# Attention, gated projection and channel MLP on one core: the values' weight conversion at one word operation a step, the exchange of halves added in place, and the last pair's reciprocals a step later

## The chip, the core and the metric

The kernel runs on one core of a Trainium2 chip. The core has a matrix engine (TensorE, PE in the profile, its weight loads PEld), a vector engine (VectorE, DVE), an engine for functions of one input (ScalarE, ACT), a general engine (GpSimd, POOL) and SyncE (SP), which here issues DMAs. Each engine works through its own queue in order; where an instruction needs another engine's result or a buffer that another still reads, it waits, and everything behind it in that queue waits too. The metric is the device time of one execution in microseconds.

## What is computed

The reference chains three blocks on two batches of 768 positions and 512 channels:

```python
q_bits = (np.einsum('bhsd,dk->bhsk', q, proj) > 0)   # 6 bits a row, the same for k
mask = q_bucket[:, :, :, None] == k_bucket[:, :, None, :]
scores = np.where(mask, scale * (q @ k.T), -1e9)
attn = exp(scores - max); attn = attn / (sum(attn) + 1e-9); x = attn @ v
...
val = x @ w_val                                       # gated by a 5-tap convolution of x
x = (gate * val) @ w_out
...
u = x + real(fft2(x)); un = normalise(u)
out = u + relu(un @ w_ch1) @ w_ch2
```

The weights (w_val, w_out, w_ch1, w_ch2, conv_w) arrive as 64-bit numbers. The kernel takes them apart by operations on their 32-bit words into a high and a low part, which TensorE multiplies one after the other.

## The kernel before

The profile has three stages: attention to about 253 us, the gated projection and the Fourier mixing to 344 us, the channel block to the end. The change is in the attention stage (function `attention`).

Attention goes over eight pairs of heads, p = 0 to 7, and in each over twelve blocks of 128 queries, i = 0 to 11 (two heads of six). A loop over n = 12p + i writes the instructions down in the order in which every engine runs them; nothing reorders them later. One turn of the loop is a step. In step n TensorE transposes the exponentials of block n (ptp), does the scores of block n + 3 (sp, four matmuls, L557), and half of a product with the values (op, L616: step by step one half of a 256-query group kb, so that one group ends every second step). VectorE clamps the scores of block n + 3 to SBUF and takes their minimum (L568), and forms the low part of the transposed exponentials (ptl, L605), after ScalarE has copied the high part (pth, L601). ScalarE also does the exponential of block n + 2 (L575).

Other work is spread over the steps i of a pair:

- `qk_beside`: at i = 1 to 3 and 9 to 11 two transposes of a later pair's queries and keys; ScalarE writes ht (L698), VectorE lt (L701). Six DMAs (L411 to L416: four qk<-ht, two qk<-lt) place them into qk at i = 3 and 9, and the next turn of ht can be written only after these have read it.
- the hash bits at i = 4 and 5: projections on TensorE (L443), signs on VectorE (L454), scaling on GpSimd (L458).
- the values of a later pair, on GpSimd at i = 5 and 11 (L174, L389, L174).
- the word operations of one half of a block of w_val (`val_weights`, through `half_weights` and `words_split`) at i = 6 to 10, in pair 0 at i = 7 to 11, in the last pair at i = 0 to 4. step0 is two operations on VectorE (L271, L272) into the PSUM tile cvp, step1 one (L275), step2 one on ScalarE and two on VectorE (L279, L280), step3 one (L283), step4 one copy on ScalarE. The tile cvp stands in the pool psm.
- the exchange of halves, at the end of each group kb (`pv_out`): two heads share the 128 partitions, and the high and low products of a head stand in different halves. ScalarE copies the group to xc (L629, two buffers), a DMA brings the other half to xs (L633, one buffer), and GpSimd adds both into xm (L634) a step after. So the DMA of a group waits for the add of the group before, and a copy to xc for the add two groups back.
- the reciprocals of the row sums (`norm_spread` on VectorE, L644; `norm_beside`: transposed on TensorE, L666, at i = 4, in the last pair at i = 1; through a DMA to rs, `norm_rows`; `norm_mul` on GpSimd, L719, at i = 10, in the last pair at i = 5).
- the convolution's products and sums of finished pairs, on GpSimd (L239, L241).

The line that says when a group is added:

```python
if kb - 1 in add and part == 0:
    add.pop(kb - 1)()
```

CW lists the steps n at which the conv weights' conversion runs.

Of the kernel before, what the change touches and what calls it, by code (L numbers as in the profile page):

```python
# [10 lines left out]
F32 = mybir.dt.float32  # L11
F32R = mybir.dt.float32r
AF = mybir.ActivationFunctionType
ALU = mybir.AluOpType
I32 = mybir.dt.int32
I64 = mybir.dt.int64

P = 128
B, H, S, D = 2, 8, 768, 64
DM = H * D  # L20
# [9 lines left out]
KSCALE = -0.125  # L30
BIG = 2.0 ** 33

CW = (2, 3, 4, 4, 5, 6, 7, 12)

WARM = (18, 3, 4)
CLAMP = BIG / 4
# [68 lines left out]
def block_kernel(  # L105
# [4 lines left out]
    nc = tc.nc  # L110
# [8 lines left out]
    col = cpool.tile([P, 6], F32, name="col")  # L119
# [60 lines left out]
    xs, gs = ExitStack(), ExitStack()  # L180
# [3 lines left out]
    g = [gpool.tile([P, NC, S + 1], F32, name=f"g{b}") for b in range(B)]  # L184
# [4 lines left out]
    wvh = xpool.tile([P, NC, DM], F32R, name="wvh")  # L189
    wvl = xpool.tile([P, NC, DM], F32R, name="wvl")  # L190
# [66 lines left out]
    ap4 = pool(raws, "ap4", side="right")  # L257
    pso = pool(ws, "pso", psum=True)
    psm = pool(ws, "psm", psum=True)
    wo_raw, wo_h, wo_l = {}, [None] * NC, [None] * NC  # L260

    def words_split(raw, dst_h, dst_l, b, a, g):

        n = raw.shape[1]
        words = raw.bitcast(I32).rearrange("p (n two) -> p n two", two=2)
        lo, hi = words[:, :, 0], words[:, :, 1]
        a, g = a.bitcast(I32), g.bitcast(I32)
        e = ap4.tile([P, DM], I32, tag="cve", name="cv")[:, :n]

        def step0():  # L270
            nc.vector.tensor_scalar(a, hi, 0x7FFFFE00, None, op0=ALU.bitwise_and)  # L271
            nc.vector.tensor_scalar(g, hi, 0x1FF, 15, op0=ALU.bitwise_and, op1=ALU.logical_shift_left)  # L272

        def step1():
            nc.vector.scalar_tensor_tensor(g, lo, 17, g, op0=ALU.logical_shift_right, op1=ALU.bitwise_or)  # L275

        def step2():
            nc.scalar.activation(a, a, AF.Relu, scale=8.0, bias=col[:, b : b + 1])
            nc.vector.scalar_tensor_tensor(a, hi, -(2 ** 31), a, op0=ALU.bitwise_and, op1=ALU.bitwise_or)  # L279
            nc.vector.tensor_scalar(e, a, -(2 ** 23), None, op0=ALU.bitwise_and)  # L280

        def step3():
            nc.vector.scalar_tensor_tensor(dst_l, g, 2.0 ** -35, e.bitcast(F32), op0=ALU.mult, op1=ALU.mult)  # L283

        def step4():
            nc.scalar.copy(dst_h, a.bitcast(F32))

        return [step0, step1, step2, step3, step4]

    def half_weights(raw, dst_h, dst_l, b):  # L290
        t = psm.tile([P, DM], F32, tag="m", name="cvp")
        n = DM // 2
        return words_split(raw, dst_h, dst_l, b, t[:, :n], t[:, n:])

    def out_load(c):

# [5 lines left out]
    def attention(es):  # L302
# [4 lines left out]
        ap2 = pool(es, "ap2", 2)  # L307
# [5 lines left out]
        NPR = len(pairs)  # L313
# [307 lines left out]
        def pv_out(kb):  # L621
            p, j, blk = kb // 6, (kb % 6) // 3, kb % 3
            if kb % 6 == 0:
                st[p]["xm"] = ap2.tile([P, S], F32, tag="xm", name="xm")
            mr = slice(64 * j, 64 * j + 64)
            cr = slice(64 - 64 * j, 128 - 64 * j)
            xc = ap2.tile([P, QB], F32, tag="xc", name="xc")
            xs = ap2.tile([P, QB], F32, tag="xs", name="xs", bufs=1)
            nc.scalar.copy(xc, po[kb])  # L629
            if kb == 6 * NPR - 1:  # L630
                nc.scalar.copy(xs[mr, :], po[kb][cr, :])
            else:
                nc.sync.dma_start(xs[mr, :], xc[cr, :])  # L633
            add[kb] = lambda: nc.gpsimd.tensor_tensor(  # L634
                st[p]["xm"][mr, blk * QB : (blk + 1) * QB], xc[mr, :], xs[mr, :], op=ALU.add
            )

        def norm_sums(p):
            sums = st[p]["sums"]
# [67 lines left out]
        def beside(p, i):  # L707

            if p + 2 < NPR and i >= 9:
                return qk_beside(p + 2, 0, i - 9)  # L710
            if 1 <= p and p + 1 < NPR and 1 <= i < 4:
                return qk_beside(p + 1, 1, i - 1)
            if 1 <= p and i == (1 if p == NPR - 1 else 4):
                return norm_beside(p - 1)

        def norm_mul(p):
# [60 lines left out]
        def val_weights(i):  # L777
            c, h = divmod(i, 2)
            cs = slice(h * DM // 2, (h + 1) * DM // 2)
            return half_weights(wv_raw[i], wvh[:, c, cs], wvl[:, c, cs], 3)  # L780

        def out_tile(i):
            t = qk_tile((0, 2, 1)[i]).rearrange("p a s -> p (a s)")
# [19 lines left out]
        for n in range(NT + 2):  # L803
# [28 lines left out]
                pv_out(kb)  # L832
            if n == 6:
                prep_step(1, i)
            if kb - 1 in add and part == 0:
                add.pop(kb - 1)()
            elif n == NT + 1:
                add.pop(kb)()
            if n == 0:
                values(0, 1)  # L840
# [8 lines left out]
            if i == 0 and p + 1 < NPR:  # L849
                load_v(p + 1)  # L850
            last = p == NPR - 1
            if i == (2 if last else 7) and 1 <= p < NPR:
                norm_rows(p - 1)
            if i == (5 if last else 10) and 1 <= p < NPR:
                norm_mul(p - 1)
            if n == NT - 1:
                early = pst.tile([P, 2, 512], F32, tag="t", name="early")
# [19 lines left out]
            elif n == NT - 2:  # L877
                norm_spread(p)

            at = 0 if last else 7 if p == 0 else 6  # L880
            if p < NPR and at <= i < at + 5:
                if i == at:
                    wsteps = val_weights(p)
                    if p + 1 < NPR:
                        val_load(p + 1)
                wsteps[i - at]()
            for _ in range(1 if n >= NT - 16 else 5 * n // 6 - 5 * (n - 1) // 6):
                if convs and n < NT and n >= min(12 * (4 * convs[0][0] + convs[0][1]) + 22, NT - 6):
                    conv_pool(*convs.pop(0), conv_tmp)
# [547 lines left out]
```

## Time and profile before

| | |
|---|---|
| time, median of three runs | 616.01 us (615.88, 616.01, 618.68) |
| profiled execution | 617.74 us, its span 616.0 us |
| TensorE busy | 603.3 us, 98% |
| VectorE busy | 444.9 us, 72% |
| ScalarE busy | 359.0 us, 58% |
| GpSimd busy | 269.7 us, 44% |

Busy shares are means over all three stages: VectorE's tenths are 9 in most of the attention stage and 1 in most of the channel stage. In the chain that ended last TensorE has 73% and VectorE 15%. A line of a timeline gives the start, the duration, the engine, the line of the kernel and the tiles; durations of consecutive instructions of one engine overlap a little, so the distance of two starts is what an instruction takes of its queue. In square brackets stands the idle time ahead of it, if any, and what ended it.

### The profile page before, as it was taken

Reading aid. Unit: us, or ns where it says so; the run is one execution under the profiler, and the core shown is the slowest. Engines: PE = TensorE matmul, PEld = TensorE weight load, DVE = VectorE, ACT = ScalarE, POOL = GpSimd, SP = SyncE. Lnnn points to the kernel's source line nnn. Section 1 sums busy time; section 2 is a strip of 40 time slices with the busy share of each in tenths; the row PEclk is TensorE's granted clock in tenths of the full one; section 3 lists DMA queues with packets and bytes.
Section 4 is the critical chain, followed back from the end, with each engine's and each line's share of the span. In section 5 each row is a group of like instructions: output and inputs, shape, how many; then the busy total and the mean of one; then the engine's idle time right before and its main releaser. Section 6 shows DMA issues by size and latency. Waiting matters only on the chain.

```text
span 616.0 us, 10435 instructions
## 1 busy us (share of the span) xinstructions
PE 603.3 (98%) x3711; PEld 539.0 (87%) x3711; DVE 444.9 (72%) x850; ACT 359.0 (58%) x712; POOL 269.7 (44%) x303
## 2 busy tenths in 40 slices
PE   8999999999999999999999999999999999999997
PEld 6889999999899989998899978888888888888886
DVE  5999999999899998799769888888886411111113
ACT  5998899998899887954625255555666111111221
POOL 7252488887798899793350632332331000000000
PEclk9999999999999999999999999999999999999999
DMA  6957585756566640162110234433440200000002
GB/s 136 219 134 171 134 185 153 173 149 158 149 159 157 196 125 14 47 257 70 36 35 0 66 122 124 135 119 122 137 136 1 103 0 1 2 0 1 0 1 102
DMA packets 54957, 62.02 MB, mean 101 GB/s; under 512 B 29184, under 2 KB 42664, under 8 KB 54650
## 3 DMA queue, kind: packets, MB, share of 16 engines
q1 hardware_dynamic: 54170, 57.81, 35.0%
q0 software_dynamic: 432, 3.55, 1.5%
q8 instruction: 29, 0.48, 0.3%
q14 instruction: 22, 0.18, 0.1%
q10 hardware_dynamic: 304, 0.01, 0.0%
HBM read 36.73 MB, written 3.19 MB: 65 GB/s over the span
## 4 chain that ended last, share of the span: by engine, by line
PE 73%; DVE 15%; ACT 3%; DMA 3%; issue 2%; SPq 2%; POOL 1%; ACTq 0%; DVEq 0%; POOLq 0%
PE pf L1344 20%; PE acc L1354 20%; PE sp L557 7%; PE op L616 6%; PE ptp L593 5%; DVE sd L568 4%; DVE ptl L605 4%; PE ps L1161 3%; PE ps L222 3%; PE ps L1225 2%; DMA qk<-ht 2%; PE late L222 1%; PE early L222 1%; PE ptp L693 1%; PE bp L443 1%
## 5 line engine op out<-in xcount | busy, mean ns | idle before, releaser
L1354 PE MATMUL acc<-w,hid 128*128 128x512 f32 x576 | 136.9, 390 | 0.0
L1354 PEld LDWEIGHTS acc<-w,hid 128*128 128x128 f32 x576 | 105.6, 188 | 19.7
L1347 DVE SCALAR_TENSOR_TENSOR hid<-pf,hid 128x512 fp32r<-128x512 f32 (+1 forms) x62 | 33.4, 557 | 119.5 <-ACT hid L1346 119.5
L1344 PE MATMUL pf<-uth,w 128*128 128x512 f32 (+1 forms) x496 | 96.7, 337 | 0.1
L568 DVE TENSOR_SCALAR_CACHE_REDUCE sd<-sp 128x768 f32<-128x768 f32 x96 | 91.2, 951 | 7.6 <-PE sp L557 7.1
L605 DVE TENSOR_TENSOR ptl<-ptp,pth 128x768 fp32r<-128x768 f32 x96 | 91.6, 954 | 5.8 <-ACT pth L601 3.8
L557 PE MATMUL sp<-qk 128*128 128x512 f32 (+1 forms) x384 | 91.5, 360 | 4.2 <-DVE sd L568 3.2
L1346 ACT ACTIVATE hid<-pf 128x512 fp32r<-128x512 f32 (+1 forms) x62 | 28.9, 488 | 114.0 <-PE pf L1344 113.9
L1344 PEld LDWEIGHTS pf<-uth,w 128*128 128x128 f32 x496 | 79.4, 188 | 14.4 <-DVE hid L1347 2.0
L575 ACT ACTIVATE sd<-sd,nm 128x768 f32<-128x768 f32 x96 | 90.1, 939 | 1.5 <-DVE sd L568 1.5
L601 ACT CAST pth<-ptp 128x768 fp32r<-128x768 f32 x96 | 77.1, 803 | 17.6 <-PE ptp L693 8.8
L162 POOL TENSOR_TENSOR w<-cv 128x512 fp32r<-128x512 f32 x31 | 40.1, 1295 | 88.7 <-DVE cv L157 77.3
L593 PE MATMUL ptp<-ident,sd 128*128 128x128 f32 x576 | 78.5, 272 | 0.2 <-ACT sd L575 0.2
L616 PE MATMUL op<-pth,v 128*128 128x256 f32 x288 | 74.0, 283 | 1.5 <-ACT xc L629 1.5
L616 PE MATMUL op<-ptl,v 128*128 128x256 f32 x288 | 73.8, 286 | 0.0
L557 PEld LDWEIGHTS sp<-qk 128*128 128x128 f32 x384 | 58.2, 189 | 13.7 <-DVE sd L568 7.3
L593 PEld LDWEIGHTS ptp<-ident,sd 128*128 128x128 f32 x576 | 65.8, 140 | 1.1 <-ACT sd L575 0.5
L634 POOL TENSOR_TENSOR xm<-xc,xs 64x256 f32<-64x256 f32 x48 | 35.3, 735 | 57.3 <-DMA xs<-xc 34.7
L616 PEld LDWEIGHTS op<-pth,v 128*128 128x128 f32 x288 | 54.1, 188 | 6.4 <-ACT xc L629 2.6
L616 PEld LDWEIGHTS op<-ptl,v 128*128 128x128 f32 x288 | 54.2, 188 | 0.3
L1344 PE MATMUL pf<-utl,w 128*128 128x512 f32 (+1 forms) x248 | 52.8, 335 | 0.0
L149 ACT ACTIVATE cv<-cv,col 128x512 int32<-128x512 int32 x32 | 23.3, 727 | 41.5 <-DVE cv L146 41.5
(214 smaller groups left out, 1000.9 us busy)
## 6 DMA issues: line engine op xcount, KB each, us to landing
raw<-in_moe_w_ch_dram SPq DMA_DIRECT2D x32, 512.0 KB
qk<-ht SPq DMA_DIRECT2D x60, 192.0 KB
qk<-lt SPq DMA_DIRECT2D x30, 192.0 KB
rqk<-in_q_dram SPq DMA_DIRECT2D x16, 192.0 KB
rqk<-in_k_dram SPq DMA_DIRECT2D x16, 192.0 KB
rv<-in_v_dram SPq DMA_DIRECT2D x8, 384.0 KB
out_dram<-o SPq DMA_DIRECT2D x12, 256.0 KB
xs<-xc SPq DMA_DIRECT2D x47, 64.0 KB
```

The lines of the kernel that those rows point to most:

```text
L162: nc.gpsimd.tensor_tensor(dst()[1], fold(g.bitcast(F32)), fold(e.bitcast(F32)), op=ALU.mult)
L557: nc.tensor.matmul(sp[:, cs], q2[i][:, m, qi * P : (qi + 1) * P], k2[i][:, m, cs], start=m == order[0], stop=m == order[1])
L568: nc.vector.tensor_scalar(sd[n], sp, CLAMP, None, op0=ALU.min, op1=ALU.min, accum_out=st[p]["nm"][:, n % 12 : n % 12 + 1],)
L575: nc.scalar.activation(sd[n], sd[n], AF.Exp, bias=st[p]["nm"][:, i : i + 1], scale=-1.0, accum_out=st[p]["sums"][:, i : i + 1],)
L593: nc.tensor.transpose(tp[:, r // 3, c0 : c0 + P], sd[n][:, r * P : (r + 1) * P], ident)
L601: nc.scalar.copy(p_parts(n)[0], tp)
L605: nc.vector.tensor_tensor(lo, tp, f32(ho), op=ALU.subtract)
L616: nc.tensor.matmul(po[kb], v3[:, r, c0 : c0 + P], pt[kb][x][:, r, :], start=r == 0 and x == 0, stop=r == R - 1 and x == 1,)
L634: add[kb] = lambda: nc.gpsimd.tensor_tensor(st[p]["xm"][mr, blk * QB : (blk + 1) * QB], xc[mr, :], xs[mr, :], op=ALU.add)
L1344: nc.tensor.matmul(pf, w[:, c, :], x[:, c, :], start=n == 0, stop=n == 3 * NC - 1)
L1347: nc.vector.scalar_tensor_tensor(hl[:, cs], pf, 0.0, f32(hh)[:, cs], op0=ALU.max, op1=ALU.subtract)
L1354: nc.tensor.matmul(acc, x[:, ts_], w, start=f == 0 and n == 0, stop=f == NF - 1 and n == 2)
```

## The change

Three edits. The word operations of w_val go through `spread_weights`: six steps instead of five, with one VectorE operation each, from i = 4 on (pair 0: 5, last pair: 0), and the sixth at the next pair's i = 0. The first two write an SBUF tile cv instead of PSUM; the third reads the raw words and cv, both in SBUF, and writes cvp in PSUM. The exchange has no tile xs: the DMA writes into xm, and GpSimd adds xc to it in place, a step later (at odd i). In the last pair the reciprocals' transpose, their spread and the multiplication come a step later, and the conv weights' last step moves from n = 12 to 13.

```diff
--- before.py
+++ after.py
@@ -30,7 +30,7 @@
 KSCALE = -0.125
 BIG = 2.0 ** 33
 
-CW = (2, 3, 4, 4, 5, 6, 7, 12)
+CW = (2, 3, 4, 4, 5, 6, 7, 13)
 
 WARM = (18, 3, 4)
 CLAMP = BIG / 4
@@ -291,6 +291,45 @@
         t = psm.tile([P, DM], F32, tag="m", name="cvp")
         n = DM // 2
         return words_split(raw, dst_h, dst_l, b, t[:, :n], t[:, n:])
+
+    def spread_weights(raw, dst_h, dst_l, b):
+
+
+        n = raw.shape[1]
+        words = raw.bitcast(I32).rearrange("p (n two) -> p n two", two=2)
+        lo, hi = words[:, :, 0], words[:, :, 1]
+        w = {}
+
+        def magnitude():
+            w["s"] = ap4.tile([P, DM], I32, tag="cve", name="cv")
+            nc.vector.tensor_scalar(w["s"][:, :n], hi, 0x7FFFFE00, None, op0=ALU.bitwise_and)
+
+        def upper():
+            nc.vector.tensor_scalar(
+                w["s"][:, n:], hi, 0x1FF, 15, op0=ALU.bitwise_and, op1=ALU.logical_shift_left
+            )
+
+        def rest():
+            t = psm.tile([P, DM], F32, tag="m", name="cvp").bitcast(I32)
+            w["a"], w["g"] = t[:, :n], t[:, n:]
+            nc.vector.scalar_tensor_tensor(
+                w["g"], lo, 17, w["s"][:, n:], op0=ALU.logical_shift_right, op1=ALU.bitwise_or
+            )
+            nc.scalar.activation(w["a"], w["s"][:, :n], AF.Relu, scale=8.0, bias=col[:, b : b + 1])
+
+        def sign():
+            nc.vector.scalar_tensor_tensor(w["a"], hi, -(2 ** 31), w["a"], op0=ALU.bitwise_and, op1=ALU.bitwise_or)
+
+        def power():
+            nc.vector.tensor_scalar(w["s"][:, :n], w["a"], -(2 ** 23), None, op0=ALU.bitwise_and)
+
+        def low():
+            nc.vector.scalar_tensor_tensor(
+                dst_l, w["g"], 2.0 ** -35, w["s"][:, :n].bitcast(F32), op0=ALU.mult, op1=ALU.mult
+            )
+            nc.scalar.copy(dst_h, w["a"].bitcast(F32))
+
+        return [magnitude, upper, rest, sign, power, low]
 
     def out_load(c):
 
@@ -625,15 +664,13 @@
             mr = slice(64 * j, 64 * j + 64)
             cr = slice(64 - 64 * j, 128 - 64 * j)
             xc = ap2.tile([P, QB], F32, tag="xc", name="xc")
-            xs = ap2.tile([P, QB], F32, tag="xs", name="xs", bufs=1)
+            to = st[p]["xm"][mr, blk * QB : (blk + 1) * QB]
             nc.scalar.copy(xc, po[kb])
             if kb == 6 * NPR - 1:
-                nc.scalar.copy(xs[mr, :], po[kb][cr, :])
+                nc.scalar.copy(to, po[kb][cr, :])
             else:
-                nc.sync.dma_start(xs[mr, :], xc[cr, :])
-            add[kb] = lambda: nc.gpsimd.tensor_tensor(
-                st[p]["xm"][mr, blk * QB : (blk + 1) * QB], xc[mr, :], xs[mr, :], op=ALU.add
-            )
+                nc.sync.dma_start(to, xc[cr, :])
+            add[kb] = lambda: nc.gpsimd.tensor_tensor(to, xc[mr, :], to, op=ALU.add)
 
         def norm_sums(p):
             sums = st[p]["sums"]
@@ -710,7 +747,7 @@
                 return qk_beside(p + 2, 0, i - 9)
             if 1 <= p and p + 1 < NPR and 1 <= i < 4:
                 return qk_beside(p + 1, 1, i - 1)
-            if 1 <= p and i == (1 if p == NPR - 1 else 4):
+            if 1 <= p and i == (2 if p == NPR - 1 else 4):
                 return norm_beside(p - 1)
 
         def norm_mul(p):
@@ -777,7 +814,7 @@
         def val_weights(i):
             c, h = divmod(i, 2)
             cs = slice(h * DM // 2, (h + 1) * DM // 2)
-            return half_weights(wv_raw[i], wvh[:, c, cs], wvl[:, c, cs], 3)
+            return spread_weights(wv_raw[i], wvh[:, c, cs], wvl[:, c, cs], 3)
 
         def out_tile(i):
             t = qk_tile((0, 2, 1)[i]).rearrange("p a s -> p (a s)")
@@ -832,9 +869,9 @@
                 pv_out(kb)
             if n == 6:
                 prep_step(1, i)
-            if kb - 1 in add and part == 0:
+            if kb - 1 in add and part == (0 if kb == 6 * NPR - 1 else 1):
                 add.pop(kb - 1)()
-            elif n == NT + 1:
+            if n == NT + 1:
                 add.pop(kb)()
             if n == 0:
                 values(0, 1)
@@ -849,9 +886,9 @@
             if i == 0 and p + 1 < NPR:
                 load_v(p + 1)
             last = p == NPR - 1
-            if i == (2 if last else 7) and 1 <= p < NPR:
+            if i == (3 if last else 7) and 1 <= p < NPR:
                 norm_rows(p - 1)
-            if i == (5 if last else 10) and 1 <= p < NPR:
+            if i == (6 if last else 10) and 1 <= p < NPR:
                 norm_mul(p - 1)
             if n == NT - 1:
                 early = pst.tile([P, 2, 512], F32, tag="t", name="early")
@@ -877,13 +914,15 @@
             elif n == NT - 2:
                 norm_spread(p)
 
-            at = 0 if last else 7 if p == 0 else 6
-            if p < NPR and at <= i < at + 5:
+            at = 0 if last else 5 if p == 0 else 4
+            if 1 <= p < NPR and i == 0:
+                wsteps.pop(0)()
+            if p < NPR and at <= i < at + (6 if last else 5):
                 if i == at:
                     wsteps = val_weights(p)
                     if p + 1 < NPR:
                         val_load(p + 1)
-                wsteps[i - at]()
+                wsteps.pop(0)()
             for _ in range(1 if n >= NT - 16 else 5 * n // 6 - 5 * (n - 1) // 6):
                 if convs and n < NT and n >= min(12 * (4 * convs[0][0] + convs[0][1]) + 22, NT - 6):
                     conv_pool(*convs.pop(0), conv_tmp)
```

On VectorE in pair 3, from the first bits operation (i = 4) on; L568 and L605 are the clamp and the low part of each step, and two word operations stand together at i = 6 and i = 8. Before:

```order
L454 TENSOR_TENSOR bits<-bp,bits 64x384
L568 TENSOR_SCALAR sd,nm<-sp 128x768
L605 TENSOR_TENSOR ptl<-ptp,pth 128x6x128
L454 TENSOR_TENSOR bits<-bp,bits 64x384
L568 TENSOR_SCALAR sd,nm<-sp 128x768
L605 TENSOR_TENSOR ptl<-ptp,pth 128x6x128
L271 TENSOR_SCALAR cvp<-wvr 128x256
L272 TENSOR_SCALAR cvp<-wvr 128x256
L568 TENSOR_SCALAR sd,nm<-sp 128x768
L605 TENSOR_TENSOR ptl<-ptp,pth 128x6x128
L275 SCALAR_TENSOR_TENSOR cvp<-wvr,cvp 128x256
L568 TENSOR_SCALAR sd,nm<-sp 128x768
```

After (L493 the bits, L607 the clamp, L644 the low part):

```order
L493 TENSOR_TENSOR bits<-bp,bits 64x384
L305 TENSOR_SCALAR cv<-wvr 128x256
L607 TENSOR_SCALAR sd,nm<-sp 128x768
L644 TENSOR_TENSOR ptl<-ptp,pth 128x6x128
L493 TENSOR_TENSOR bits<-bp,bits 64x384
L308 TENSOR_SCALAR cv<-wvr 128x256
L607 TENSOR_SCALAR sd,nm<-sp 128x768
L644 TENSOR_TENSOR ptl<-ptp,pth 128x6x128
L315 SCALAR_TENSOR_TENSOR cvp<-wvr,cv 128x256
L607 TENSOR_SCALAR sd,nm<-sp 128x768
L644 TENSOR_TENSOR ptl<-ptp,pth 128x6x128
```

Each step has now one word operation: magnitude (L305), upper (L308), rest (L315) and sign (L321), the first two ahead of where the conversion began before.

On VectorE at the start of the last pair, around the reciprocals (rinv). Before:

```order
L568 TENSOR_SCALAR sd,nm<-sp 128x768
L605 TENSOR_TENSOR ptl<-ptp,pth 128x6x128
L644 RECIPROCAL rinv<-sums 128x12
L271 TENSOR_SCALAR cvp<-wvr 128x256
L272 TENSOR_SCALAR cvp<-wvr 128x256
L568 TENSOR_SCALAR sd,nm<-sp 128x768
L605 TENSOR_TENSOR ptl<-ptp,pth 128x6x128
L275 SCALAR_TENSOR_TENSOR cvp<-wvr,cvp 128x256
```

After:

```order
L607 TENSOR_SCALAR sd,nm<-sp 128x768
L644 TENSOR_TENSOR ptl<-ptp,pth 128x6x128
L681 RECIPROCAL rinv<-sums 128x12
L327 SCALAR_TENSOR_TENSOR wvl<-cvp,cv 128x256
L305 TENSOR_SCALAR cv<-wvr 128x256
L607 TENSOR_SCALAR sd,nm<-sp 128x768
L644 TENSOR_TENSOR ptl<-ptp,pth 128x6x128
L308 TENSOR_SCALAR cv<-wvr 128x256
L607 TENSOR_SCALAR sd,nm<-sp 128x768
L644 TENSOR_TENSOR ptl<-ptp,pth 128x6x128
```

The reciprocals keep their place and two word operations beside them: the sixth of pair 6 (L327) and the first of this pair (L305); the steps after have one.

On GpSimd in pair 2, around the multiplication L719 (xT<-xm,rs) at i = 10; L634 is the add, L640 the sums, conv_tmp and g_73 are the convolution's products and sums. Before:

```order
L634 TENSOR_TENSOR xm<-xc,xs 64x256
L241 TENSOR_TENSOR g_73<-g_73,conv_tmp 128x768
L640 TENSOR_SCALAR sums<-sums 128x12
L634 TENSOR_TENSOR xm<-xc,xs 64x256
L719 TENSOR_TENSOR xT_72<-xm,rs 128x6x128
L239 TENSOR_SCALAR g_73<-xT_72,cwt 128x768
L174 TENSOR_SCALAR v_1581<-rv 128x6x64
L389 TENSOR_TENSOR v_1581<-rv,v_1581 128x6x64
L174 TENSOR_SCALAR v_1581<-v_1581 128x6x64
L239 TENSOR_SCALAR conv_tmp<-xT_72,cwt 128x768
L634 TENSOR_TENSOR xm<-xc,xs 64x256
```

After (L673 the add, L756 the multiplication, L428 the values' addition):

```order
L673 TENSOR_TENSOR xm<-xc,xm 64x256
L241 TENSOR_TENSOR g_73<-g_73,conv_tmp 128x768
L673 TENSOR_TENSOR xm<-xc,xm 64x256
L677 TENSOR_SCALAR sums<-sums 128x12
L756 TENSOR_TENSOR xT_72<-xm,rs 128x6x128
L239 TENSOR_SCALAR g_73<-xT_72,cwt 128x768
L673 TENSOR_TENSOR xm<-xc,xm 64x256
L174 TENSOR_SCALAR v_1562<-rv 128x6x64
L428 TENSOR_TENSOR v_1562<-rv,v_1562 128x6x64
L174 TENSOR_SCALAR v_1562<-v_1562 128x6x64
L239 TENSOR_SCALAR conv_tmp<-xT_72,cwt 128x768
```

The adds come at other places between the other operations: one of them now follows the multiplication and the convolution's product, ahead of the values (L174, L428).

## Rows read from the trace of the kernel before

**Rows 1.** Windows: length; PE, PEld, DVE, ACT, POOL busy us (instructions); clock, DMA share, GB/s
```profile
119.00:148.00 29.00, 28.71 (x219) 27.20 (x218) 27.75 (x54) 26.17 (x55) 22.46 (x25) 1.00 0.71 170
215.00:241.00 26.00, 25.07 (x189) 23.48 (x188) 24.39 (x48) 21.32 (x44) 24.07 (x23) 1.00 0.31 79
```

**Rows 2.** Timeline, TensorE: start, duration, instruction, [idle before, what ended it]
```profile
123.44 0.82 PE L593 MATMUL ptp<-ident,sd 128*128 128x128 f32 x6
...
147.22 0.82 PE L593 MATMUL ptp<-ident,sd 128*128 128x128 f32 x6
...
149.28 0.82 PE L593 MATMUL ptp<-ident,sd 128*128 128x128 f32 x6
150.38 0.97 PE L557 MATMUL sp<-qk 128*128 128x512 f32 x4 [0.29 <-DVE sd L568]
...
151.94 0.82 PE L593 MATMUL ptp<-ident,sd 128*128 128x128 f32 x6
```

**Rows 3.** Timeline, VectorE, 148 to 152 us
```profile
148.59 0.42 DVE L271 TENSOR_SCALAR cvp<-wvr 128x256 int32<-128x256 int32 x1
...
149.37 0.95 DVE L568 TENSOR_SCALAR_CACHE_REDUCE sd<-sp 128x768 f32<-128x768 f32 x1
...
151.11 0.42 DVE L275 SCALAR_TENSOR_TENSOR cvp<-wvr,cvp 128x256 int32<-128x256 int32 x1
151.44 0.95 DVE L568 TENSOR_SCALAR_CACHE_REDUCE sd<-sp 128x768 f32<-128x768 f32 x1
```

**Rows 4.** Timelines, TensorE and, last, ScalarE, 161 to 168 us
```profile
161.16 0.82 PE L593 MATMUL ptp<-ident,sd 128*128 128x128 f32 x6
...
163.45 0.81 PE L593 MATMUL ptp<-ident,sd 128*128 128x128 f32 x6
...
166.51 0.39 PE L616 MATMUL op<-pth,v 128*128 128x256 f32 x1 [1.32 <-ACT xc L629]
...
167.33 0.82 PE L593 MATMUL ptp<-ident,sd 128*128 128x128 f32 x6
...
164.80 0.47 ACT L698 ACTIVATE ht<-ptp,col 128x256 fp32r<-128x256 f32 x1 [1.77 <-DMA qk<-ht]
```

**Rows 5.** Timeline, SyncE, 126 to 159 us: DMA issues
```profile
126.93 0.48 SPq L633 DMA_DIRECT2D xs<-xc  x1
...
158.17 0.48 SPq L633 DMA_DIRECT2D xs<-xc  x1
158.70 0.60 SPq L411 DMA_DIRECT2D qk<-ht  x1
```

**Rows 6.** Timeline, GpSimd, 157 to 164 us
```profile
157.41 0.73 POOL L634 TENSOR_TENSOR xm<-xc,xs 64x256 f32<-64x256 f32 x1 [3.36 <-DMA xs<-xc]
...
163.04 0.91 POOL L239 TENSOR_SCALAR g<-xT,cwt 128x768 f32<-128x768 f32 x1
```

**Rows 7.** Timeline, TensorE, last pair
```profile
221.44 0.27 PE L666 MATMUL ptp<-ident,rinv 128*12 128x128 f32 x1 [0.68 <-DVE rinv L644]
```

**Rows 8.** Timelines of the channel stage, VectorE and, last, GpSimd
```profile
360.41 1.51 DVE L146 TENSOR_SCALAR cv<-raw 128x512 int32<-128x512 int32 x1 [0.23 <-ACT w L169]
...
365.71 0.42 DVE L146 TENSOR_SCALAR cv<-raw 128x512 int32<-128x512 int32 x1
...
360.36 1.28 POOL L162 TENSOR_TENSOR w<-cv 128x512 fp32r<-128x512 f32 x1 [2.58 <-DVE cv L157]
```

**Rows 9.** Groups by line and form: instruction xcount, busy us, mean ns, idle us before
```profile
L1054 DVE TENSOR_TENSOR gt<-g 128x384 f32<-128x384 f32 x8 | 6.5, 849 | 2.4 <-POOL gl L1062 2.4
L1054 DVE TENSOR_TENSOR gt<-g,late 128x384 f32<-128x384 f32 x8 | 4.2, 552 | 0.3 <-POOL xT L719 0.2
```

**Rows 10.** Timelines of pair 1, VectorE and, last, GpSimd
```profile
61.21 0.96 DVE L568 TENSOR_SCALAR_CACHE_REDUCE sd<-sp 128x768 f32<-128x768 f32 x1 [0.22 <-PE sp L557]
...
63.09 0.42 DVE L271 TENSOR_SCALAR cvp<-wvr 128x256 int32<-128x256 int32 x1
...
62.32 1.02 POOL L389 TENSOR_TENSOR v<-rv,v 128x384 fp32r<-128x384 f32 x1
```

## The prediction

> **What bounds the kernel now.** I read the windows first. In the middle of the attention stage TensorE is busy 28.71 of 29.0 us, VectorE 27.75, ScalarE 26.17, GpSimd 22.46 [rows 1]. So TensorE sets the time, but VectorE has only 1.25 us to spare in that stretch, and wherever one step gives VectorE a little more than the others it passes TensorE. TensorE's own instructions stay the same in number and kind, so the change can only win idle time of TensorE, or add some. I therefore looked next at TensorE's timeline for steps that are longer than their kind.
>
> A plain step (i = 6 to 8 of a pair: six transposes, four score matmuls, six value matmuls) takes 2.06 us (147.22 to 149.28). Step i = 8 takes 2.66 (149.28 to 151.94), and its scores start with an idle of 0.29 us that the clamp on VectorE ends [rows 2]. The reason stands on VectorE's timeline: at i = 6 it does two word operations of the conversion, 148.59 to 149.37 or 0.78 us, where a single one takes 0.33 (151.11 to 151.44). With one of them, the clamps are 2.07 us apart (149.37 to 151.44) [rows 3]; with two that makes 2.52, against TensorE's 2.06. And TensorE can't wait this out: a clamp (0.95 us) stands between the scores of one step (0.97) and those of the next, and with the hand-overs this ring fills a plain step to within an estimated 0.07 us. The same 0.60 us is lost in each of pairs 1 to 6, and in pair 6 a second time (0.49), with two word operations again.
>
> The largest single stall is elsewhere. Step 62 (163.45 to 167.33) takes 3.88 us, the one before it, of the same kind, 2.29 (161.16 to 163.45): TensorE waits 1.32 us behind ScalarE, whose rewrite of ht has waited 1.77 us until the copies qk<-ht had read it [rows 4]. Those copies were issued late. SyncE's queue is in order, and ahead of them stood xs<-xc, issued at 158.17; the first of the four qk<-ht followed at 158.70. 158.17 is 6.23 us after step 57's start (151.94); a pair earlier xs<-xc went out at 126.93 [rows 5], 3.49 us after the start of the same step (123.44 [rows 2]). It was late because the one xs buffer comes free only when GpSimd has added the exchange before, and that add started at 157.41, after 3.36 us of waiting for its own transfer [rows 6].
>
> In the last pair TensorE idles 0.68 us for the reciprocals [rows 7]; GpSimd is busy 24.07 of 26 us there and VectorE 24.39 [rows 1].
>
> **The change part by part.** The sum is made against the profiled execution, 617.74 us (span 616.0 and 1.74 around it); the median of the three runs is 616.01, and the gain is taken off that at the end.
>
> Conversion, pairs 1 to 5. The same six word operations per pair come one a step, at i = 4 to 8, the sixth at the next pair's i = 0. At i = 4 and 5 TensorE has the projections besides; VectorE waits 0.22 us for scores there (61.21 [rows 10]), so a word of 0.33 makes that clamp 0.11 late, in a step whose extra matmuls cover it: nothing. At i = 6 to 8 VectorE needs 2.07 against 2.06: nearly even. Uncontended, the whole 0.60 us per pair goes, 3.0 in five pairs.
>
> But magnitude, upper and rest now work between SBUF tiles, where before every word operation had an operand in PSUM. What that may cost is shown by the channel stage: the same tensor_scalar (L146, twice as wide) takes 0.42 us when GpSimd is idle, and 1.51 when it starts beside GpSimd's L162 (1.28 us, from 360.36) [rows 8]. A VectorE operation with two SBUF inputs (L1054) takes 849 ns, with one of them in PSUM 552 [rows 9]. In a pair, magnitude and upper directly follow a bits operation, whose result GpSimd mostly waits for. Rest comes at the place of L271 now, 63.09 in pair 1, while GpSimd's value addition L389 runs from 62.32 to 63.34 [rows 10]. So it waits 0.25 us, some 0.4 where GpSimd is 0.15 later; less the 0.07 that is forgiven, I take 0.30 given back in each pair, and 0.30 won. Bounds: 0.60 won, or a block like the 1.51 - 0.42 = 1.09 of rows 8, which gives 0.60 - 1.02 = -0.42. Sum 1.5 (3.0 to -2.1); I take the value that the overlap at this very place gives.
>
> The Trainium skill, page "SBUF — State Buffer", section "Who interferes with whom", speaks against this part. It says that VectorE shares one pair of SBUF ports with GpSimd, that a VectorE operation in a two-port mode, or one with two SBUF inputs beside a GpSimd operation that reads SBUF, contends for it, and that the later of the two then waits for the whole instruction. Rows 8 and 9 agree (1.51 us against 0.42, 849 ns against 552). By the rule this term is the 1.5 above; were it not to reach these operations, 3.0.
>
> Pair 6: the same 0.30, and the second stall of 0.49 (its two word operations at i = 8 become one). 0.8, from -0.4 to 1.1.
>
> Pair 0: the operations move by two steps within a pair in which VectorE converts the conv weights' words as well, and no step is freed as a whole. 0, from -0.6 to 0.6 (one step's stall either way).
>
> Exchange. The transfer goes straight into xm, which has two buffers, so it waits only for ScalarE's copy xc and no more for the add. The DMA and the add stay the same in size. Its successor then goes out as in the earlier pair, some 3.5 us after step 57's start instead of 6.2, the four qk<-ht behind it as well, and the 1.77 us wait goes: step 62 gives 3.88 - 2.29 = 1.6. Three smaller stalls after it (step 64, and steps 74 to 76 of pair 6) lose 0.6 in all in the same way. Sum 2.2 (0 if something else holds the queue). What is late next: xc has two buffers, so a copy waits for the add two exchanges back, and with that add a step later two steps are left, not three; see the slow rival. The load wvr, issued two steps earlier, stands ahead of two bits copies on SyncE: one issue of about 0.5 us, covered, since these wait for GpSimd's bits.
>
> Last pair. The reciprocals' transpose moves from step 85 to 86, so the reciprocal has a step more, but beside it VectorE still does two word operations (low and magnitude). The 0.68 falls to about 0.25; the two later stalls of 0.42 (the picture of rows 2, in steps 88 and 91) to 0.65 together, since at i = 5 there are now three word operations. 1.52 becomes 0.90: 0.6 won. Against that, magnitude, upper and rest run beside a GpSimd that is busy 93% of the time, and VectorE has nothing to spare; with products and sums of 0.9 to 1.9 us in flight each waits an estimated 0.5 (half of 1.09), 1.5 in all. 0.6 - 1.5 is -0.9; with the 7% in which GpSimd is idle, -0.8; bounds -2.6 (three blocks of 1.09) and +0.6. The normalising multiplication moves from i = 5 to 6; its product is wanted a stage later. The conv weights' transpose moves by one step: nothing.
>
> Sum: 1.5 + 0.8 + 0 + 2.2 - 0.8 = 3.7. 617.74 becomes 614.0; on the median, 616.01 - 3.7 = 612.3.
>
> **The rivals.**
> No contention (609.1): the SBUF operands cost nothing, so 3.0 + 1.1 + 2.2 + 0.6 = 6.9. For it: in pairs 1 to 6 GpSimd idles 6.5 of 29 us [rows 1], and 0.2 us more or less decides whether rest meets L389. Against it: rows 8 to 10.
>
> Contention takes it all (615.8): rest is held so long that step 8's stall only moves to step 6 or 7, and the last pair loses 2.0; only the 2.2 of the exchange stay. For it: the 0.07 us that the ring forgives. Against it: the overlap of 0.25 us in rows 10.
>
> The exchange doesn't reach ht (614.5): qk<-ht stays late, because ScalarE's copy or the transfers themselves hold it. 1.5 + 0.8 - 0.8 = 1.5. Against it: the add's 3.36 us wait [rows 6] stands right ahead of the late issue.
>
> Slower (620.1): GpSimd's lag now holds ScalarE. The add of i = 11 comes behind the normalising multiplication and a convolution product (L239); in pair 4 that product starts at 163.04 and ends at 163.95, the add 0.73 later: 164.7 [rows 6]. ScalarE's copy that needs this add's buffer ended just ahead of TensorE's 166.51 [rows 4]; without the stall of 1.6 it would start near 164.5. So in that pair the slack is used up, and each further lag of GpSimd is ScalarE's and then TensorE's. If GpSimd, held by VectorE's new SBUF operations in its turn, is 1.3 us later in each of pairs 1 to 6, that is 7.8, less 3.7: 4.1 slower. Against it: pair 4's lag comes itself from the late transfers, and GpSimd has idle time to catch up.
>
> **How the numbers follow.** Forecast 0.40, no contention 0.22, contention takes it all 0.24, exchange without effect 0.07, slower 0.07. A measurement tells 0.5%, 3.1 us, from no change: below 612.9 is faster, above 619.1 slower. The forecast's own range is 610.8 to 613.8, some 0.7 of it under 612.9: 0.28; with 0.21 of the no-contention case and 0.02 of the others, faster is 0.51; slower is 0.06 of its rival and 0.01 of the contention case; same 0.42. The range for 8 in 10 reaches from just under the no-contention case to 1 us beyond the case in which contention takes all: 608.8 to 616.8.
>
> **What would show it.** Right: step i = 8 of pairs 1 to 6 at 2.1 to 2.4 us; step 62 at 2.3 and no wait of ht's rewrite for qk<-ht; rest longer than 0.42 us and ending after L389; in the last pair magnitude or upper at 0.9 us and more. Wrong: if these three last 0.33 to 0.42 throughout (no contention), if step 62 stays at 3.9, or if ScalarE's copy xc waits for GpSimd's add (the slower case).

## The result and the profile after

The changed kernel takes 622.37 us (median of 6 runs, 621.62 to 622.42), the kernel before 617.35 (median of 6). The ratio is 1.0085, 95% interval 1.0065 to 1.0106: slower by some 5 us, where 3.7 us faster was forecast, and above the range's upper end of 616.8. The profiled execution took 622.39 us, its span 620.4.

Where the time went shows in two windows, the attention stage and the rest (columns as in [rows 1]). After:

```profile
core 0: us, PE busy (x) PEld busy (x) DVE busy (x) ACT busy (x) POOL busy (x), PEclk, DMA share, GB/s
14.00:257.40 243.40, 233.81 (x1725) 216.74 (x1724) 224.21 (x422) 210.14 (x429) 172.88 (x191) 1.00 0.60 147
257.40:620.40 363.00, 358.61 (x1930) 311.10 (x1928) 214.71 (x415) 140.00 (x272) 88.19 (x76) 1.00 0.20 67
```

And before:

```profile
14.00:253.00 239.00, 233.49 (x1727) 218.46 (x1727) 222.61 (x422) 211.14 (x429) 170.55 (x192) 1.00 0.61 151
253.00:616.00 363.00, 358.65 (x1931) 311.26 (x1929) 215.93 (x415) 140.37 (x272) 88.19 (x76) 1.00 0.20 67
```

Both second windows are the last 363 us of their span, and TensorE is busy equally long in them (358.61 and 358.65 us); the last block's transposes start at 250.02 us, before the change at 245.75. So the attention stage grew, by 4.3 to 4.4 us, and in it no engine got more to do to speak of: TensorE is busy 233.8 us against 233.5, VectorE 224.2 against 222.6, ScalarE 210.1 against 211.1. So it is waiting, and the waits name it (engine and line that waited, us in total, how often, the longest):

```profile
engine line waited for: us in total, times, longest us
ACT cvp L318 <- DVE cvp L315: 11.7, 8, 2.3
...
ACT wvh L330 <- DVE wvl L327: 8.5, 8, 1.2
...
PE op L655 <- ACT xc L668: 6.6, 13, 0.7
```

In the kernel before, neither the Relu nor the copy to wvh waited in any of the eight conversions of w_val. Now ScalarE waits some 1.5 us in each (0.9 to 2.3) for rest (L315) ahead of its Relu (L318), and 1.1 us for low (L327) ahead of the copy to wvh (L330). TensorE's 6.6 us behind ScalarE's copy xc were 1.5 before:

```profile
PE op L616 <- ACT xc L629: 1.5, 2, 1.3
```

This answers to [rows 2, 3]: the steps i = 7 and 8 of pair 4. ScalarE after:

```profile
149.72 0.94 ACT L614 ACTIVATE sd<-sd,nm 128x768 f32<-128x768 f32 x1
...
152.21 0.48 ACT L318 ACTIVATE cvp<-cv,col 128x256 int32<-128x256 int32 x1 [1.46 <-DVE cvp L315]
152.62 0.79 ACT L640 CAST pth<-ptp 128x768 fp32r<-128x768 f32 x1
...
154.24 0.36 ACT L668 COPY xc<-op 128x256 f32<-128x256 f32 x1
```

ScalarE has begun the exponential written in step 6 at 149.72, ends it, and is then idle for 1.46 us, until the Relu can start. Step 7's pth and exponential follow that much later, and so does the copy xc (154.24). VectorE after, in the same stretch:

```profile
149.40 0.30 DVE L308 TENSOR_SCALAR cv<-wvr 128x256 int32<-128x256 int32 x1
...
150.56 0.95 DVE L644 TENSOR_TENSOR ptl<-ptp,pth 128x768 fp32r<-128x768 f32 x1
151.43 0.68 DVE L315 SCALAR_TENSOR_TENSOR cvp<-wvr,cv 128x256 int32<-128x256 int32 x1
...
153.44 0.96 DVE L644 TENSOR_TENSOR ptl<-ptp,pth 128x768 fp32r<-128x768 f32 x1 [0.46 <-ACT pth L640]
```

Each step has one word operation now, as meant. Rest (L315) ends at 152.11, and the Relu begins 0.1 us after it. Later VectorE itself waits 0.46 us for the pth that ScalarE delivered late. TensorE after:

```profile
150.19 0.82 PE L632 MATMUL ptp<-ident,sd 128*128 128x128 f32 x6
...
152.25 0.82 PE L632 MATMUL ptp<-ident,sd 128*128 128x128 f32 x6
...
154.65 0.38 PE L655 MATMUL op<-pth,v 128*128 128x256 f32 x1 [0.65 <-ACT xc L668]
...
155.46 0.82 PE L632 MATMUL ptp<-ident,sd 128*128 128x128 f32 x6
```

The step takes 3.21 us (152.25 to 155.46) where it took 2.66 [rows 2], and the idle is at another place: no longer at the scores, which a clamp released, but 0.65 us at the value matmuls, released by ScalarE's copy xc. The same picture stands at i = 2, where pairs 2 to 4 had no stall before. ScalarE and TensorE after, in step 62:

```profile
166.14 0.37 ACT L330 CAST wvh<-cvp 128x256 fp32r<-128x256 f32 x1 [1.06 <-DVE wvl L327]
166.41 0.81 ACT L640 CAST pth<-ptp 128x768 fp32r<-128x768 f32 x1
167.10 0.49 ACT L735 ACTIVATE ht<-ptp,col 128x256 fp32r<-128x256 f32 x1
```

```profile
166.68 0.82 PE L632 MATMUL ptp<-ident,sd 128*128 128x128 f32 x6
...
168.82 0.38 PE L655 MATMUL op<-pth,v 128*128 128x256 f32 x1 [0.41 <-ACT xc L668]
...
169.63 0.82 PE L632 MATMUL ptp<-ident,sd 128*128 128x128 f32 x6
```

The step takes 2.95 us (166.68 to 169.63) in pairs 2 to 6. For step 62 this is less than the 3.88 of [rows 4], since the exchange did what it should; SyncE after:

```profile
158.91 0.48 SPq L672 DMA_DIRECT2D xm<-xc  x1
159.49 0.54 SPq L450 DMA_DIRECT2D qk<-ht  x1
```

The transfer goes out 3.45 us after step 57's start (155.46 above), where it was 6.23 [rows 5]. In the last pair the idle for the reciprocals [rows 7] is gone, and one of 0.42 us for the clamp stands in the next step instead:

```profile
226.48 0.98 PE L596 MATMUL sp<-qk 128*128 128x512 f32 x4 [0.42 <-DVE sd L607]
```

### The profile page after: what moved, and what is told of

It is laid out like the page before. It is cut to its first block, busy times and chain, and to the rows that moved or that the text cites. A ratio compares the mean times of both kernels' runs of the same rounds, so it can differ in the third digit from the quotient of the medians.

```text
span 620.4 us, 10402 instructions
## 1 busy us (share of the span) xinstructions
PE 603.6 (97%) x3711; PEld 537.0 (87%) x3711; DVE 445.8 (72%) x850; ACT 357.6 (58%) x712; POOL 272.5 (44%) x303
## 4 chain that ended last, share of the span: by engine, by line
PE 74%; DVE 11%; ACT 7%; issue 3%; SPq 2%; DMA 2%; POOL 0%; ACTq 0%; POOLq 0%; DVEq 0%
PE pf L1383 20%; PE acc L1393 19%; PE op L655 8%; PE sp L596 6%; PE ptp L632 5%; PE ps L1200 3%; PE ps L222 3%; PE ps L1264 2%; ACT sd L614 2%; DVE ptl L644 2%; DVE sd L607 2%; ACT pth L640 2%; PE late L222 1%; PE bp L482 1%; PE early L222 1%
## 5 line engine op out<-in xcount | busy, mean ns | idle before, releaser
L644 DVE TENSOR_TENSOR ptl<-ptp,pth 128x768 fp32r<-128x768 f32 x96 | 91.5, 953 | 11.1 <-ACT pth L640 7.4
L607 DVE TENSOR_SCALAR_CACHE_REDUCE sd<-sp 128x768 f32<-128x768 f32 x96 | 91.3, 952 | 5.3 <-PE sp L596 3.9
L640 ACT CAST pth<-ptp 128x768 fp32r<-128x768 f32 x96 | 77.4, 806 | 5.2 <-PE ptp L632 2.6
L673 POOL TENSOR_TENSOR xm<-xc,xm 64x256 f32<-64x256 f32 x48 | 35.2, 733 | 31.8 <-DMA xm<-xc 21.6
L241 POOL TENSOR_TENSOR g<-g,conv_tmp 128x768 f32<-128x768 f32 x27 | 46.9, 1736 | 1.3
```

Of the source, the lines that this page charges most:

```text
L241: nc.gpsimd.tensor_tensor(dst, dst, tmp, op=ALU.add)
L607: nc.vector.tensor_scalar(sd[n], sp, CLAMP, None, op0=ALU.min, op1=ALU.min, accum_out=st[p]["nm"][:, n % 12 : n % 12 + 1],)
L640: nc.scalar.copy(p_parts(n)[0], tp)
L644: nc.vector.tensor_tensor(lo, tp, f32(ho), op=ALU.subtract)
L673: add[kb] = lambda: nc.gpsimd.tensor_tensor(to, xc[mr, :], to, op=ALU.add)
```

## The experiments

Three theories stood against each other. O: the loss is the order on ScalarE; its two instructions of the conversion now stand behind VectorE's last operation of the same step, and wait because both touch the PSUM tile cvp. K: the loss is contention of the new SBUF operands with GpSimd. X: the add a step later holds ScalarE's copy xc. All ratios are to the kernel before, run on the same chip.

**1. ScalarE's instruction ahead of VectorE's, in both steps.** The changed kernel with two swaps in `spread_weights`:

```diff
 def rest():
+    nc.scalar.activation(w["a"], w["s"][:, :n], AF.Relu, ...)
     nc.vector.scalar_tensor_tensor(w["g"], lo, 17, w["s"][:, n:], ...)
-    nc.scalar.activation(w["a"], w["s"][:, :n], AF.Relu, ...)
 def low():
+    nc.scalar.copy(dst_h, w["a"].bitcast(F32))
     nc.vector.scalar_tensor_tensor(dst_l, w["g"], ...)
-    nc.scalar.copy(dst_h, w["a"].bitcast(F32))
```

> The changed kernel, with ScalarE's two parts of the conversion written ahead of VectorE's part of the same step (Relu ahead of rest at i = 6, the copy to wvh ahead of low at i = 0); nothing else differs. Theory O (order on ScalarE: its Relu and copy stand behind VectorE's last operation of the same step, because both touch the PSUM tile cvp): steps i = 8 fall from 3.2 to 2.1 us (6 x 1.1), steps i = 2 from 2.95 to 2.3 (5 x 0.65), the last pair gives about 0.9, so some 611 us against 622.4. Theory K (the SBUF operands' contention with GpSimd makes the loss): 621 to 622. Theory X (the exchange's add a step later holds ScalarE's copy xc): 621 to 622.

Measured: 612.38 us, ratio 0.9933 (0.9915 to 0.9952). Both waits are gone from the list. ScalarE, then TensorE, of this kernel at the same steps:

```profile
144.39 0.94 ACT L614 ACTIVATE sd<-sd,nm 128x768 f32<-128x768 f32 x1
...
145.32 0.47 ACT L315 ACTIVATE cvp<-cv,col 128x256 int32<-128x256 int32 x1
145.72 0.80 ACT L640 CAST pth<-ptp 128x768 fp32r<-128x768 f32 x1
```

```profile
146.91 0.81 PE L632 MATMUL ptp<-ident,sd 128*128 128x128 f32 x6
...
147.70 0.96 PE L596 MATMUL sp<-qk 128*128 128x512 f32 x4
...
149.27 0.82 PE L632 MATMUL ptp<-ident,sd 128*128 128x128 f32 x6
```

VectorE:

```profile
146.09 0.69 DVE L316 SCALAR_TENSOR_TENSOR cvp<-wvr,cv 128x256 int32<-128x256 int32 x1
```

The Relu follows the exponential at once, and rest (L316 here) waits for nothing, since ScalarE is ahead of VectorE by then. Step 8 takes 2.36 us, step 2 the plain 2.29. K and X are out as the cause of the loss: neither the operands nor the exchange differ between the two kernels, and their times differ by 10.0 us. By steps: 6 x 0.85 at i = 8, 5 x 0.66 at i = 2, 0.4 each in pairs 0 and 1, and 0.9 in the last pair.

**2. Only the Relu first.**

> The changed kernel with only the Relu ahead of rest. O: steps i = 8 at 2.1 us, steps i = 2 still at 2.95; some 615 us. K and X: 621 to 622.

Measured: 616.83 us, ratio 1.0007 (0.9995 to 1.0020). Steps 8 are at 2.36 us (2.46 in pair 5), steps 2 at 2.95. The steps are as O has them; the total came 1.8 us higher than my estimate, which had counted the whole of step 8's excess, down to 2.1.

**3. Only the copy first.**

> The changed kernel with only the copy to wvh ahead of low. O: steps i = 2 at 2.3 us, steps i = 8 still at 3.2; some 618.5 us. K and X: 621 to 622.

Measured: 618.20 us, ratio 1.0024 (1.0009 to 1.0039). Steps 2 are at 2.29, steps 8 at 3.21. The two waits add up, within the noise: 622.4 - 5.5 (from the second experiment) - 4.2 (from this) is 612.7, and both together gave 612.4.

**4. Only the exchange.** The kernel before with the second edit of the change alone.

```diff
-nc.sync.dma_start(xs[mr, :], xc[cr, :])
+nc.sync.dma_start(to, xc[cr, :])          # to: the place in xm
...
+add[kb] = lambda: nc.gpsimd.tensor_tensor(to, xc[mr, :], to, op=ALU.add)
...
-if kb - 1 in add and part == 0:
+if kb - 1 in add and part == (0 if kb == 6 * NPR - 1 else 1):
```

> The kernel before, with only the exchange changed (transfer straight into xm, add in place and a step later). The prediction's term: step 62's stall of 1.6 us and three small ones go, 2.2 us under the kernel before, ratio 0.9964. Theory X: the later add holds ScalarE's copy xc, the same or slower than before (ratio 1.000 or more). O and K say nothing of it.

Measured: 615.52 us, ratio 0.9982 (0.9971 to 0.9994); the profiled execution is 2.0 us under the profiled one of before (615.72 against 617.74). SyncE and TensorE of this kernel:

```profile
155.31 0.48 SPq L633 DMA_DIRECT2D xm<-xc  x1
155.90 0.54 SPq L411 DMA_DIRECT2D qk<-ht  x1
```

```profile
163.35 0.82 PE L593 MATMUL ptp<-ident,sd 128*128 128x128 f32 x6
...
165.64 0.82 PE L593 MATMUL ptp<-ident,sd 128*128 128x128 f32 x6
```

xm<-xc is issued at 155.31 and step 62 takes 2.29 us. The steps 62 and 64 give 1.8 together, as predicted; of the other stalls one stays (step 74, 2.52). So X is out by itself. The ratio confirms a gain, its size between 0.4 and 1.8 us, less than the 2.2 expected. The runs of the kernel before on this chip lie between 615.46 and 618.92, this kernel's between 615.27 and 616.56, and the traced execution of before (617.74) is in the upper part: whether the stall of step 62 stands in all its executions, no run shows.

**5. The Relu early in the kernel before.** The same wait made in a kernel that has neither the spread conversion nor SBUF operands nor the new exchange:

```diff
 def step1():
     nc.vector.scalar_tensor_tensor(g, lo, 17, g, ...)
+    nc.scalar.activation(a, a, AF.Relu, ...)
 def step2():
-    nc.scalar.activation(a, a, AF.Relu, ...)
```

> The kernel before, with one line moved: ScalarE's Relu of the conversion stands behind step1's VectorE operation (i = 7) instead of one step later (i = 8); everything stays in PSUM, the exchange is the old one. Theory O (ScalarE waits for VectorE's last operation of the same step): ScalarE idles some 1.4 us there and TensorE loses about 1 us a pair, some 622 us. Theory K (only SBUF operands of VectorE cost time): unchanged, 616.5.

Measured: 622.48 us, ratio 1.0086 (1.0067 to 1.0106). One line is worth as much as the whole change. ScalarE of this kernel:

```profile
151.94 0.36 ACT L629 COPY xc<-op 128x256 f32<-128x256 f32 x1
153.86 0.45 ACT L276 ACTIVATE cvp<-cvp,col 128x256 int32<-128x256 int32 x1 [1.56 <-DVE cvp L275]
154.24 0.81 ACT L601 CAST pth<-ptp 128x768 fp32r<-128x768 f32 x1
```

1.56 us of idle, released by L275, and in each of pairs 1 to 6 the step i = 10 is 0.5 to 0.8 us longer (2.85 us against 2.33 in pair 1); pair 0 adds 1.0, steps 84 to 94 another 1.0 and what follows them 1.5, where w_out is converted by the same steps. Step 62's stall of 1.6 is not there, although the exchange is the old one. So the order alone makes such a loss, and by the first experiment the loss goes with it.

**6. The last pair's reciprocals back at their old steps.** The first experiment's kernel with the third edit undone, except for the conv weights' step.

> The first experiment's kernel with the last pair's reciprocals back at their old steps (transpose at i = 1, spread at 2, multiplication at 5). The prediction's term: 0.4 us of the 0.68 idle come back, 612.8 against 612.4. If three VectorE operations at i = 0 set the loss wherever the transpose stands, no change within 0.2 us.

Measured: 611.91 us, ratio 0.9913 (0.9895 to 0.9931), against 612.38 in another set of runs; the spans differ by 0.3 us (610.0 and 610.3). Within that it changes nothing. TensorE waits at the reciprocals again:

```profile
215.22 0.28 PE L703 MATMUL ptp<-ident,rinv 128*12 128x128 f32 x1 [0.69 <-DVE rinv L681]
```

but in the first experiment's kernel the clamps behind VectorE's words take as much: steps 84 to 91 make 18.6 us in both.

**7. Upper in PSUM.** The first experiment's kernel; cvp is taken at i = 5, behind the bits.

```diff
 def upper():
-    nc.vector.tensor_scalar(w["s"][:, n:], hi, 0x1FF, 15, ...)
+    t = psm.tile([P, DM], F32, tag="m", name="cvp").bitcast(I32)
+    w["a"], w["g"] = t[:, :n], t[:, n:]
+    nc.vector.tensor_scalar(w["g"], hi, 0x1FF, 15, ...)
 def rest():
-    nc.vector.scalar_tensor_tensor(w["g"], lo, 17, w["s"][:, n:], ...)
+    nc.vector.scalar_tensor_tensor(w["g"], lo, 17, w["g"], ...)
```

> The first experiment's kernel with upper writing into the PSUM tile cvp again, taken at i = 5 behind the bits, so that rest has one SBUF input and upper is no operation between SBUF tiles. Theory K' (rest is held by GpSimd's addition of the values, 0.27 us at i = 6, and upper 0.9 us in the last pair): rest lasts 0.42 us, steps i = 8 fall from 2.37 to 2.1 (6 x 0.27), the last pair gives 0.7; some 610.1 against 612.4. If the remaining 0.3 us of steps i = 8 is VectorE's load alone (2.07 us a step): 612.4.

Measured: 610.83 us, ratio 0.9894 (0.9874 to 0.9914), the span 1.3 us shorter (609.0). The groups of upper and rest by line (instruction xcount, busy us, mean ns, idle us before), first of the first experiment's kernel, then of this:

```profile
L316 DVE SCALAR_TENSOR_TENSOR cvp<-wvr,cv 128x256 int32<-128x256 int32 x8 | 5.0, 626 | 0.0
L308 DVE TENSOR_SCALAR cv<-wvr 128x256 int32<-128x256 int32 x8 | 3.3, 408 | 0.2
```

```profile
L310 DVE TENSOR_SCALAR cvp<-wvr 128x256 int32<-128x256 int32 x8 | 3.4, 426 | 0.2
L316 DVE SCALAR_TENSOR_TENSOR cvp<-wvr,cvp 128x256 int32<-128x256 int32 x8 | 3.3, 418 | 0.0
```

With SBUF operands rest takes 626 ns in the mean, with one of them in PSUM 418, and steps 8 fall from 2.36 to 2.12 us. That GpSimd makes rest long, and not the form of its operands, shows in the first experiment's kernel: where GpSimd's L428 is under way, in pairs 1 to 6, rest takes 0.68 to 0.75 us (146.09 above), in pair 0 and the last pair, without it, 0.41 and 0.42. GpSimd beside the rest of pair 4, then VectorE in pair 0:

```profile
145.47 1.02 POOL L428 TENSOR_TENSOR v<-rv,v 128x384 fp32r<-128x384 f32 x1
```

```profile
36.29 0.41 DVE L316 SCALAR_TENSOR_TENSOR cvp<-wvr,cv 128x256 int32<-128x256 int32 x1
```

The 408 ns of upper hide two kinds: 0.30 us in seven pairs, and 1.19 us in the last, beside a busy GpSimd; in PSUM the mean is 426, the longest 428. That one upper, in the first experiment's kernel:

```profile
217.29 1.19 DVE L308 TENSOR_SCALAR cv<-wvr 128x256 int32<-128x256 int32 x1
```

So K is a true cost, 0.24 us a pair, but a small one. (Step 7 takes 0.03 more, 2.09, in pair 5 0.13.)

**8. The last two pairs' words spread further.**

> The seventh experiment's kernel with the conversion of the last two pairs spread further: pair 6's low at i = 9, the last pair's magnitude and upper at pair 6's i = 10 and 11, the rest at i = 1 to 4, so that no step but i = 5 (the first of w_out) has more than one word operation. The stalls of steps 86 (0.4) and 91 (0.8, of which half goes) shrink: 0.8 us under the seventh, some 609.3. If GpSimd and not VectorE sets the last pair: no change.

Measured: 610.54 us, ratio 0.9891 (0.9871 to 0.9911). The time is 0.3 us under the seventh kernel's, where 0.8 was expected; the intervals overlap. Steps 86 and 91 fell by 0.9 together, but step 84 rose from 2.08 to 2.77. GpSimd, then VectorE, of this kernel:

```profile
208.84 1.86 POOL L756 TENSOR_TENSOR xT<-xm,rs 128x768 f32<-128x768 f32 x1 [0.32 <-DMA rs<-rd]
```

```profile
209.75 1.10 DVE L305 TENSOR_SCALAR cv<-wvr 128x256 int32<-128x256 int32 x1
210.77 0.94 DVE L607 TENSOR_SCALAR_CACHE_REDUCE sd<-sp 128x768 f32<-128x768 f32 x1
```

Magnitude, still an operation between SBUF tiles, starts at 209.75 in the middle of GpSimd's multiplication and ends 0.15 us after it.

**9. That magnitude in PSUM.** The eighth kernel, with the tile cvp taken a step earlier in the last pair and the Relu in place.

> The eighth experiment's kernel with the last pair's magnitude in the PSUM tile cvp as well (Relu in place). Theory K' for a single operation: in the eighth magnitude lasts 1.10 us at 209.75, held until GpSimd's multiplication (208.84, 1.86 us) has ended, and step 84 takes 2.77 us; with a PSUM destination it lasts 0.42 us and step 84 takes 2.1, so 0.7 us less, some 609.9 against 610.5. If magnitude was long for another reason, step 84 stays at 2.77.

Measured: 609.98 us, ratio 0.9888 (0.9866 to 0.9911); the span is 608.4 against 608.9. Magnitude takes 0.42 us (L308 here), though it starts in the middle of the same multiplication (L763 here), and step 84 takes 2.08. GpSimd, then VectorE, of this kernel:

```profile
209.47 1.86 POOL L763 TENSOR_TENSOR xT<-xm,rs 128x768 f32<-128x768 f32 x1 [0.51 <-DMA rs<-rd]
```

```profile
209.89 0.42 DVE L308 TENSOR_SCALAR cvp<-wvr 128x256 int32<-128x256 int32 x1
```

This is the fastest version, 6.6 us under the kernel before and some 12 under the change; against the seventh and eighth the intervals overlap.

**10. Contention away, order kept.** The changed kernel with the seventh experiment's edit, the Relu and the copy where the change has them.

> The changed kernel with upper in the PSUM tile cvp (so that rest has one SBUF input), and ScalarE's Relu and copy where the change has them, behind VectorE's operation of the same step. Theory O: rest 0.25 us shorter lets the Relu start that much earlier, steps i = 8 some 2.95 instead of 3.2, steps i = 2 stay at 2.95; 620 to 621. Theory K (contention makes the loss): under 616.

Measured: 621.60 us, ratio 1.0078 (1.0057 to 1.0098). ScalarE of this kernel:

```profile
150.83 0.48 ACT L318 ACTIVATE cvp<-cv,col 128x256 int32<-128x256 int32 x1 [1.25 <-DVE cvp L315]
```

Steps 8 are at 2.99 us and steps 2 at 2.95: the contention gone and the loss still there. Rest no longer touches cv in this kernel, so cvp is the only tile that it shares with the Relu, and the wait is still 1.25 us. With the first experiment this closes the square: the order is worth 10.0 us with upper in SBUF (622.4 to 612.4) and 10.8 with it in PSUM (621.6 to 610.8), the operands 0.8 and 1.5. The four stand on different chips, on which the kernel before differs by up to 0.9 us, so the 0.8 alone is not clear of the noise.

## Why the prediction was wrong

The step that failed is "The change part by part", the paragraph "Conversion, pairs 1 to 5". It counted the six word operations on VectorE, their place and their contention, and gave ScalarE's two instructions of the conversion no place and no price. They are the same two instructions of 0.4 us as before, which is why they looked free. But before the change the Relu stood one step behind the operation ahead of it in the conversion, and the copy too, so that VectorE was long done in all eight pairs. Now both stand in the step of VectorE's operation, behind it, and VectorE does its word operation as the last thing of a step, after clamp and low part, when ScalarE has been ahead by some 1.4 us. The Relu needs only magnitude, two steps old, and the copy only sign; they wait all the same, because they touch the tile cvp that rest writes and low reads, and two engines' accesses to one PSUM tile are made to follow each other as they are written down: the first experiment only swaps them, and then it is VectorE that would have to wait, and ScalarE is early. The Trainium skill, page "PSUM — Partial Sum Buffer", section "PSUM bank collisions raise a hardware error", says that the compiler's back end puts a dependency between any two instructions of different engines on the same PSUM bank and the same quarter of partitions, reads and writes alike; these runs agree, with 1.06 us of wait between low and the copy, which both only read the tile; whether the tile or its whole bank is what counts, no run here separates. The order of the instructions on ScalarE, set beside VectorE's, could have shown it. The prediction looked at VectorE's and GpSimd's order alone.

The rival on the slower side had the place where TensorE would wait (the value matmuls, behind ScalarE's copy xc) and the sign, at 620.1 with a chance of 0.07, but the wrong cause: it was not GpSimd's lag, and in the profile after ScalarE's copy xc waits for GpSimd only once, 0.6 us. The mechanism that happened had no chance in the prediction at all. Of the signs that the prediction named, two came: rest is longer than 0.42 us and ends after L428, and the rewrite of ht no longer waits for qk<-ht. Steps 8 and 62, put at 2.1 to 2.4 and 2.3 us, took 3.21 and 2.96, and magnitude in the last pair, put at 0.9 and more, 0.73 in the changed kernel.

Term by term, the rest can be read from the kernels without that wait:

- Contention of rest: 0.30 given back in each pair was forecast. Rest is 0.25 us longer (0.68 against 0.42, beside GpSimd's L428 in [rows 10]'s place), and step 8 stays at 2.36 us with it and 2.12 without: 0.24. Right.
- Conversion in pairs 1 to 6, 2.3 forecast, some 3.5 measured: step 8 gives 0.30 as said, and steps 10, 11 and 0 another 0.27 a pair that the prediction had not seen (2.33, 2.40 and 2.19 before, 2.29, 2.29 and 2.07 after). The forecast was too small.
- Pair 0, 0 forecast: steps 7 to 14, over which its operations reach, take 19.71 us in the kernel before and in the first experiment's. Right.
- Pair 6's second stall: gone, 2.56 to 2.08. Right.
- Exchange, 2.2 forecast: 2.0 in the profiled execution, 0.4 to 1.8 by the runs. Right in mechanism, too large in size: the term was read from an execution of 617.74 us and taken off a median of 616.01.
- Last pair, -0.8 forecast: -0.25 in the first experiment (steps 84 to 91, 18.39 before, 18.64), with upper at 1.19 us and the three operations at i = 5 as named. In the changed kernel itself -1.1, with the waits of ScalarE in it. Right in kind, and 0.5 too pessimistic. The reciprocals' move is worth nothing, where 0.4 was put on it.

The kernel without the wait took 612.38 us against the forecast's 612.3. That closeness is luck in part: the conversion gave 1.2 us more than its term and the last pair 0.5, the exchange by the runs some 1.2 less, and the kernel before took 616.47 on that chip, not the 616.01 that the forecast started from.

## What to carry to other kernels

When a sequence over several engines is cut into finer steps, list for each engine which instruction its own now follows within a step, and what that instruction's engine still has ahead of it; an instruction that keeps its length can lose a step of slack. Where two engines work on halves of one PSUM tile, write the instruction of the engine that runs ahead first: here two such swaps are worth 10 us of 622. An operation of VectorE between SBUF tiles should not stand where GpSimd is busy, even if it is the shorter one alone.

## What was not expected of the hardware

Alone, the word operations between SBUF tiles are shorter than those with a PSUM operand: magnitude and upper take 0.29 us for 128x256 elements, where 0.42 was usual with a PSUM destination. Beside GpSimd the same ones took 1.10 and 1.19 us. And the block goes both ways: rest held GpSimd's instruction behind it, the third of the values' three (L174), which took 0.69 us in the changed kernel (at 151.79) and 0.51 in the seventh experiment's, where rest has a PSUM input.
